# Moving when ScalarE's Silus run in a fused attention and feed-forward kernel, fixing ScalarE's order, and moving the state's decay to VectorE

## The chip, the cores and the metric

The kernel runs on one NeuronCore of one Trainium2 chip. The metric is the device time of one execution in microseconds (us), and I quote medians over several executions. Every execution that is compared here was in the fast state (no profile or time of a slower state came up).

The profile lists the work by engine. Four matter here, with their busy time before the change: TensorE for matrix products ("PE", 615.1 us, its weight loads listed apart as "PEld", 495.8 us), VectorE ("DVE", 498.4 us), ScalarE ("ACT", 286.6 us) and GpSimd ("POOL", 29.9 us). The trace shows for each its own sequence of instructions, and its waits for the others: ScalarE's Silus, for one, waited 30.9 us for sums of VectorE (L731).

## The reference

```python
def _attn_ref(q, k, v, f_logit):                     # batch 4, 8 heads, 768 steps, 48 per head
    f = 1.0 / (1.0 + np.exp(-f_logit))
    state = np.zeros((B, H, D, D), dtype=np.float32)
    for t in range(S):
        state = f[:, :, t, :, None] * state + np.einsum('bhd,bhe->bhde', k[:, :, t], v[:, :, t])
        y[:, :, t] = np.einsum('bhd,bhde->bhe', q[:, :, t], state)

def _moe_ref(x, w_gate, w_val, w_out):               # 3072 tokens, 384 -> 1536 -> 384
    g = x @ w_gate
    silu = g * (1.0 / (1.0 + np.exp(-g)))
    return silu * (x @ w_val) @ w_out
```

The attention's output, as 3072 rows of 384, is the x of the feed-forward block. All is float32.

## The kernel before

The sequence of 768 is cut into six chunks of 128 steps. The feed-forward part of chunk 0 multiplies plainly. Chunks 1 to 5 use two fast schemes that trade products for sums: a *triple* forms six gate/value blocks with fifteen products (four triples a chunk), and the output is formed with seven products. While the feed-forward part of chunk c runs, the attention of chunk c+1 (four batches) is worked off beside it; chunk 5 has none beside it.

Three places matter. The first is the attention step with the decay of the state and the Sigmoid of the gates:

```python
        if c >= SQUARES:
            nc.scalar.activation(squares("f"), squares("f"), AF.Sigmoid)                      # L510
        ...
        nc.vector.tensor_tensor_scan(tail[:, 0:n][:, ::-1], gate[:, 0:n][:, ::-1], ...)       # L519
        ...
            nc.gpsimd.tensor_tensor(decayed[:, :, 0:D], states[b], whole.broadcast_to(...), ALU.mult)   # L544
```

`decayed` is read by TensorE, and `whole`, the decay's factor, is a slice of the tile that the next scan writes; so that scan (L519) has to wait until the decay has read it (8 such waits in the trace, 5.0 us in all, the longest 0.69).

The second is the triple. `product(r)` makes two matmul calls, which the trace shows as four matmuls, into one of the PSUM banks A, B, o, c; bank B has one buffer and A has two, so a later product has to wait until ScalarE has copied the bank out (the trace has 8 such waits for B's copies into `aside`, 8.5 us in all, and 20 for A's, 6.5 us). `finish` applies Silu on ScalarE and then the product with the value half on VectorE:

```python
    def chained(made, f):
        n = len(traced)
        f()
        mine = [ins for ins in traced[n:] if ins.engine == mybir.EngineType.PE]
        keep_order(made[-1:] + mine)
        made.extend(mine)
    ...
        def triple(j):
            made, p, got = [], {}, {}
            ...
            def copy(name, tag, **kw):
                t = comb.tile([128, 2, TH], FP32, tag=tag, name=tag, **kw)
                nc.scalar.copy(t, p[name])
                return t

            def aside(name):
                return copy(name, "aside", bufs=3)

            def finish(i, n, src):
                dst = out_part(i, n, j)
                nc.scalar.activation(dst, src[:, 0, :], AF.Silu)
                nc.vector.tensor_tensor(dst, dst, src[:, 1, :], ALU.mult)

            def some(n, m):
                for r in range(n, m):
                    product(r)
                    if r == 0:
                        got[11] = copy("A", "c11", bufs=2)
                    # ... r = 1 to 4 cut: copies and sums
                    elif r == 5:
                        minus(got[12], p["o"], got[12])
                        finish(0, 1, got[12])
                    elif r == 6:
                        minus(got[22], got[22], aside("A"))
                        finish(1, 1, got[22])
                    # ... r = 7 to 11 cut
                    elif r == 12:
                        minus(got[31], got[31], aside("A"))
                        finish(2, 0, got[31])
                    elif r == 13:
                        plus(got[11], got[11], aside("B"))
                        finish(0, 0, got[11])
                    else:
                        finish(1, 0, p["A"])

            return [lambda n=n: chained(made, lambda: some(n, n + 5)) for n in (0, 5, 10)]
```

The third thing is that a scheduler of the compiler orders each engine's instructions before the run, from its own model of times. `keep_order` forbids it to reorder the instructions of the list; before the change that holds TensorE's products within a triple, and nothing on ScalarE.

Of the kernel before, what the change touches and what calls it, by code (L numbers as in the profile page):

```python
# [12 lines left out]
AF = mybir.ActivationFunctionType  # L13
ALU = mybir.AluOpType
# [275 lines left out]
def short_path(ctx, tc, ident, least, judge, q, k, v, f_logit, moe_w_gate, moe_w_val, moe_w_out, out):  # L290
# [9 lines left out]
    nc = tc.nc  # L300
    B, H, S, D = q.shape
    C = 128
    NCH = S // C
    HP = H // 2
# [57 lines left out]
    def pairs(t, off=0):  # L362
        return t[:, off:off + HP * N1].rearrange("p (a t) -> p a t", t=N1)
# [7 lines left out]
    states = [const.tile([128, HP, D], FP32, tag=f"state{b}", name=f"state{b}") for b in range(B)]  # L371

    decayed = const.tile([128, HP, W], FP32, tag="decayed", name="decayed")
# [114 lines left out]
    def rows_of(par):  # L488
        return slice(W * par, W * par + D)
# [6 lines left out]
    def attention(u):  # L496
        b, c = units[u]
# [4 lines left out]
        def transposed(name, src):  # L502
            p = bank(name)
            for a in range(HP):
                nc.tensor.transpose(p[:, a * C:(a + 1) * C],
                                    src[:, 2 * a:2 * a + 2, :].rearrange("t r d -> t (r d)"), ident)
            return p.rearrange("p (a t) -> p a t", t=C)
# [4 lines left out]
        else:  # L512
            p = transposed("fTp", fr)
# [4 lines left out]
        n = HP * N1  # L518
        nc.vector.tensor_tensor_scan(tail[:, 0:n][:, ::-1], gate[:, 0:n][:, ::-1], ones[:, ::-1], 1.0,  # L519
                                     op0=ALU.mult, op1=ALU.add)  # L520
        whole = pairs(tail)[:, :, 1:2]
# [19 lines left out]
        if c:  # L541
            if c < SQUARES:
                load_after(u)
            nc.gpsimd.tensor_tensor(decayed[:, :, 0:D], states[b], whole.broadcast_to((128, HP, D)), ALU.mult)  # L544
        yield

        A = att.tile([128, 2, HP, C], FP32, tag="A", name="A")
# [1 line left out]
        for a in range(HP):  # L549
            for par in range(2):  # L550
                r = rows_of(par)
# [4 lines left out]
        if c < NCH - 1:  # L556
            p = bank("kt")
# [8 lines left out]
        if c:  # L566
# [8 lines left out]
            for a in range(HP):  # L575
                for par in range(2):
                    r = rows_of(par)
# [9 lines left out]
            for h in range(H):  # L587
                a, par = h // 2, h % 2
                f = h * D
                while f < (h + 1) * D:  # L590
                    n = min((h + 1) * D, (f // 128 + 1) * 128) - f
                    r = W * (a % 2) + f - h * D
# [10 lines left out]
        if c < NCH - 1:  # L603
            p = bank("dS")
# [11 lines left out]
        if not c:  # L616
            p = bank("xTp")
# [5 lines left out]
    def load_after(u):  # L623

        w = u + (1 if units[u][1] >= SQUARES else 2)
        if w < len(units) and (units[w][1] >= SQUARES) == (w == u + 1):
            load(w)
# [8 lines left out]
    traced = nc.cur_bb.bb.instructions  # L636
# [9 lines left out]
    def keep_order(mine):  # L646
        for a, b in zip(mine, mine[1:]):
            tc.add_manual_dep(b, a.name, mybir.DependencyInfo(mybir.DependencyClass.NoSync,
                                                              mybir.DependencyReason.DATA), reason="order")
# [123 lines left out]
    def chained(made, f):  # L773

        n = len(traced)
        f()
        mine = [ins for ins in traced[n:] if ins.engine == mybir.EngineType.PE]
        keep_order(made[-1:] + mine)
        made.extend(mine)


    PRODUCTS = [("A", "a11", "t14"), ("B", "a23", "t8"), ("o", "a21", "b22"),
# [4 lines left out]

    def mlp_fifteen(c):
        h = {}
        b11, b12, b21, b22, b31, b32 = (xT[c][:, k, n * TH:(n + 1) * TH] for k in range(KT) for n in range(2))  # L790
        tokens = dict(b11=b11, b21=b21, b22=b22, b32=b32, t3=b31, t10=b12)

        def token_sums():
            x = comb.tile([128, 9, TH], FP32, tag="xs", name="xs")
            for n, nm in enumerate(("t14", "t15", "t8", "t9", "t2", "t1", "t4", "t11", "t5")):
                tokens[nm] = x[:, n, :]
            t = tokens
            minus(t["t14"], b21, b31)
            minus_both(t["t15"], b31, b32)
            plus(t["t8"], b21, t["t15"])  # L800
            plus(t["t9"], b12, b22)
            minus_both(t["t2"], t["t9"], t["t14"])
            plus(t["t1"], b12, b32)
            minus(t["t5"], b32, b11)
            plus(t["t4"], b11, t["t9"])
            minus_both(t["t11"], t["t4"], b21)
            plus(b12, b11, b12)
            plus(b31, b11, b31)

        w, e = weight_parts()  # L810
        weights_of = {f"a{i + 1}{k + 1}": t for (i, k), t in w.items()}
        weights_of.update({f"e{n}": t for n, t in enumerate(e)})

        def out_part(i, n, j):
            f = i * NJ + j
            if f % NP not in h:
                h[f % NP] = hidden_tile()
            return h[f % NP][:, 2 * (f // NP) + n, :]

        def triple(j):  # L820
            cols = slice(j * 128, (j + 1) * 128)
            made, p, got = [], {}, {}

            def both(name):
                return {"A": banks_a, "B": banks_b, "o": banks_o, "c": banks_o}[name].tile(
                    [128, 512], FP32, tag=name if name in "AB" else "o", name=name).rearrange("p (n t) -> p n t", n=2)

            def product(r):
                name, a, b = PRODUCTS[r]
                fresh = name == "o" or name not in p  # L830
                if fresh:
                    p[name] = both(name)
                for n in range(2):
                    nc.tensor.matmul(p[name][:, n, :], lhsT=weights_of[a][:, n, cols], rhs=tokens[b],  # L834
                                     start=fresh and n == 0, stop=True, skip_group_check=True)
# [8 lines that stand above are left out]

            def finish(i, n, src):

                dst = out_part(i, n, j)
                nc.scalar.activation(dst, src[:, 0, :], AF.Silu)  # L848
                nc.vector.tensor_tensor(dst, dst, src[:, 1, :], ALU.mult)  # L849

            def some(n, m):
                for r in range(n, m):
# [3 lines that stand above are left out]
                    elif r == 1:  # L856
                        got[22] = copy("B", "c22")
                    elif r == 2:
                        minus(got[22], p["o"], got[22])
                    elif r == 3:  # L860
                        got[12] = copy("A", "c12")
                    elif r == 4:
                        plus(got[12], got[12], aside("B"))
                    elif r == 5:
                        minus(got[12], p["o"], got[12])
                        finish(0, 1, got[12])
                    elif r == 6:
                        minus(got[22], got[22], aside("A"))
                        finish(1, 1, got[22])
                    elif r == 7:  # L870
                        got[32] = copy("B", "c32")
                    elif r == 8:
                        got[31] = copy("c", "c31")
                    elif r == 9:
                        plus(got[32], got[32], aside("A"))
                    elif r == 10:
                        minus(got[31], got[31], aside("B"))
                    elif r == 11:
                        minus(got[32], got[32], p["c"])
                        finish(2, 1, got[32])  # L880
# [5 lines that stand above are left out]
                        finish(0, 0, got[11])  # L886
                    else:
                        finish(1, 0, p["A"])

            return [lambda n=n: chained(made, lambda: some(n, n + 5)) for n in (0, 5, 10)]  # L890

        hidden_sums, last = down_seven(c, h)
        order = list(range(0, NJ, 2)) + list(range(1, NJ, 2))
        pieces = [token_sums] + [f for j in order for f in triple(j)]
        half = 1 + 3 * (NJ // 2)
        ready = [sorted({(i * NJ + j) % NP for i in range(KT) for j in range(n, NJ, 2)}) for n in range(2)]
        pieces.insert(half, lambda: [hidden_sums(n) for n in ready[0]])
        pieces.append(lambda: [hidden_sums(n) for n in ready[1]])
        return pieces, last

    def down_seven(c, h):
# [163 lines left out]
    for c in range(NCH):  # L1065
        if c == 0:
# [5 lines left out]
            pieces = hidden + weave(last, weight_sums(0))  # L1072
        else:
            hidden, last = mlp_fifteen(c)
            if c == 1:
                half = len(hidden) // 2
                hidden = hidden[:1] + weave(hidden[1:half], weight_sums(1)) + hidden[half:]
                hidden.append(lambda: behind(down_weight_sums))
            pieces = hidden + last
# [86 lines left out]
```

## Time and profile before

| | before |
|---|---|
| time, median | 644.23 us (643.03 to 645.19, 4 runs) |
| span of the profiled execution | 641.5 us |
| chunk 1 (fifteen-product part, seven-product part) | 105.9 (71.9, 34.0) us |
| chunk 2 | 102.6 (69.8, 32.9) us |
| chunk 3 | 102.2 (68.5, 33.7) us |
| chunk 4 | 96.3 (64.3, 32.0) us |
| chunk 5 | 80.1 (52.1, 28.0) us |

The lengths of the chunks are read between fixed landmarks of the trace: a chunk starts at the last output matmul of the chunk before it, and its two parts are divided at the first matmul of the seven-product scheme. This gives the same cut in every kernel, so the parts can be compared from run to run.

The table of busy time in stretches, for the fifteen-product parts of chunks 1 to 4 before the change (columns: stretch, length, then busy us of PE, PEld, DVE, ACT and POOL with counts, granted clock, DMA share, GB/s):

```profile
148.90:220.80 71.90, 66.85 (x447) 54.74 (x445) 70.80 (x127) 46.85 (x87) 1.86 (x3) 1.00 0.34 88
254.80:324.60 69.80, 66.09 (x444) 54.03 (x442) 55.51 (x100) 45.03 (x84) 1.34 (x2) 1.00 0.27 69
357.40:425.90 68.50, 65.43 (x443) 53.68 (x441) 55.26 (x99) 39.58 (x79) 1.03 (x2) 1.00 0.23 59
459.60:523.90 64.30, 62.11 (x383) 50.89 (x381) 53.07 (x99) 35.51 (x74) 1.82 (x3) 1.00 0.18 46
```

Take length minus PE for chunks 2 to 4: 3.71 + 3.07 + 2.19 = 8.97 us in which TensorE has nothing in it. In chunk 1 it is 5.05 us, and there VectorE is busy 70.80 of 71.90.

The group of the Silus, from the groups by line on ScalarE (after the last bar: idle time of ScalarE just before them, and for what):

```profile
L848 ACT ACTIVATE h<-c 128x256 f32<-128x256 f32 x100 | 40.4, 416 | 34.8 <-DVE c L731 30.9 <-DVE c L728 2.7
```

ScalarE stands 34.8 us in front of Silus whose input VectorE hasn't finished. A copy behind such a Silu stands as well: the one at 305.81 us starts after a Silu that has stood 3.57 us, though the matmuls of its product ended at 302.10.

### The profile page before, as it was taken

What the parts mean: (1) busy time and instruction counts of PE and PEld (TensorE: products, weight loads), DVE (VectorE), ACT (ScalarE), POOL (GpSimd) and SP (SyncE); (2) the same over time, 40 slices, a digit from 0 to 9 for tenths busy, and PEclk for the clock granted to TensorE, in tenths of its full rate; (3) what the DMA queues carried; (4) which work ended last, traced back from release to release, by engine and by line L of the source; (5) the groups of instructions that cost most, each with busy time, mean ns of one, the idle gap of its engine ahead of it and who ended that gap; (6) DMA issues with size and microseconds to landing.
All of it is one profiled execution on the core that took longest, in us unless ns stands there. A gap on an engine that the chain in (4) does not pass through costs nothing.

```text
span 641.5 us, 10613 instructions
## 1 busy us (share of the span) xinstructions
PE 615.1 (96%) x3894; PEld 495.8 (77%) x3894; DVE 498.4 (78%) x921; ACT 286.6 (45%) x526; POOL 29.9 (5%) x42
## 2 busy tenths in 40 slices
PE   7999999999998999999899999899999999999996
PEld 4954545667777799887689887689887789988896
DVE  6888879959999997679897589897679893467741
ACT  1474646205666511874640465461165540165600
POOL 1000000000000050000020000020000000000000
PEclk8999999999999999999999999999999999999999
DMA  9997475006133414113332313223402300100001
GB/s 176 216 221 239 118 188 172 14 17 190 30 83 92 98 44 113 43 40 80 79 79 71 99 29 84 62 67 87 120 26 50 75 9 7 62 1 1 0 1 54
DMA packets 98396, 51.90 MB, mean 81 GB/s; under 512 B 56864, under 2 KB 92192, under 8 KB 98336
## 3 DMA queue, kind: packets, MB, share of 16 engines
q1 hardware_dynamic: 95024, 46.63, 30.9%
q10 hardware_dynamic: 3312, 4.52, 2.0%
q8 instruction: 32, 0.52, 0.4%
q14 instruction: 28, 0.23, 0.1%
HBM read 42.47 MB, written 4.72 MB: 74 GB/s over the span
## 4 chain that ended last, share of the span: by engine, by line
PE 60%; DVE 19%; SPq 7%; DMA 5%; ACT 3%; issue 3%; POOL 0%; DVEq 0%; ACTq 0%; POOLq 0%
PE o L923 13%; PE A L834 9%; PE B L834 8%; SPq L593 5%; PE gate L666 5%; PE val L666 5%; PE sc L552 3%; PE o L834 3%; PE o L690 3%; DVE c L731 3%; PE c L834 2%; PE o L977 2%; PE y L582 2%; DMA ksquares<-in_k_dram 2%; DVE tails L519 1%
## 5 line engine op out<-in xcount | busy, mean ns | idle before, releaser
L834 PE MATMUL A<-xs,w_both 128*128 128x256 f32 x240 | 63.1, 383 | 3.6 <-ACT c L839 2.4
L923 PE MATMUL o<-w_out,h 128*128 128x192 f32 x360 | 62.6, 330 | 0.9 <-DVE w_out L731 0.4
L728 DVE TENSOR_TENSOR c<-c,aside 128x512 f32<-128x512 f32 x60 | 41.9, 698 | 26.8 <-ACT aside L839 26.7
L923 PEld LDWEIGHTS o<-w_out,h 128*128 128x128 f32 x360 | 58.1, 190 | 2.8 <-DVE w_out L731 0.6
L848 ACT ACTIVATE h<-c 128x256 f32<-128x256 f32 x100 | 40.4, 416 | 34.8 <-DVE c L731 30.9
L839 ACT COPY c<-A 128x512 f32<-128x512 f32 x40 | 23.3, 584 | 69.3 <-DMA out_dram<-ob 25.9
L839 ACT COPY aside<-A 128x512 f32<-128x512 f32 x60 | 35.2, 586 | 42.3 <-PE A L834 42.3
L834 PEld LDWEIGHTS A<-xs,w_both 128*128 128x128 f32 x240 | 44.2, 190 | 11.6 <-ACT c L839 4.1
L544 POOL TENSOR_TENSOR decayed<-state,tails 128x192 f32<-128x192 f32 x20 | 27.0, 1351 | 480.4 <-DVE state L610 331.7
L834 PE MATMUL B<-xs,w_both 128*128 128x256 f32 x160 | 42.6, 388 | 6.2 <-ACT aside L839 5.7
L731 DVE TENSOR_TENSOR c<-c,aside 128x512 f32<-128x512 f32 x60 | 41.7, 696 | 5.8 <-ACT aside L839 5.6
L849 DVE TENSOR_TENSOR h<-h,c 128x256 f32<-128x256 f32 x100 | 40.8, 421 | 5.9 <-ACT h L848 5.7
L834 PE MATMUL B<-xT,extra 128*128 128x256 f32 x160 | 41.3, 380 | 0.2 <-ACT aside L839 0.2
L834 PE MATMUL c<-xT,w_both 128*128 128x256 f32 x160 | 41.1, 379 | 0.0
L834 PE MATMUL A<-xs,extra 128*128 128x256 f32 x160 | 41.1, 379 | 0.0
L923 PE MATMUL o<-ws,h 128*128 128x192 f32 x240 | 40.9, 326 | 0.0
L839 ACT COPY aside<-B 128x512 f32<-128x512 f32 x60 | 35.0, 583 | 13.1 <-PE B L834 13.1
L923 PEld LDWEIGHTS o<-ws,h 128*128 128x128 f32 x240 | 39.1, 190 | 0.1
L834 PEld LDWEIGHTS B<-xs,w_both 128*128 128x128 f32 x160 | 29.0, 190 | 12.4 <-ACT aside L839 7.5
L519 DVE TENSOR_TENSOR_SCAN tails<-gates,ones 128x516 f32<-128x516 f32 x24 | 29.3, 1222 | 9.2 <-POOL decayed L544 5.0
L731 DVE TENSOR_TENSOR c<-o,c 128x512 f32<-128x512 f32 x40 | 27.8, 696 | 10.6 <-PE o L834 8.8
L552 PEld LDWEIGHTS sc<-qT,kT 48*128 48x128 f32 x384 | 25.0, 187 | 14.0 <-issue 10.0
(132 smaller groups left out, 1196.4 us busy)
## 6 DMA issues: line engine op xcount, KB each, us to landing
fsquares<-in_f_logit_dram SPq DMA_DIRECT2D x64, 96.0 KB, 2.4
ksquares<-in_k_dram SPq DMA_DIRECT2D x64, 96.0 KB, 2.4
qsquares<-in_q_dram SPq DMA_DIRECT2D x64, 96.0 KB, 2.4
v<-in_v_dram SPq DMA_DIRECT2D x24, 192.0 KB, 3.6
w<-in_moe_w_gate_dram SPq DMA_DIRECT2D x6, 768.0 KB, 4.6
w<-in_moe_w_val_dram SPq DMA_DIRECT2D x6, 768.0 KB, 5.4
w<-in_moe_w_out_dram SPq DMA_DIRECT2D x6, 768.0 KB, 5.4
out_dram<-ob ACTq DMA_DIRECT2D x23, 192.0 KB, 2.6
```

Of the source, the lines that this page charges most:

```text
L519: nc.vector.tensor_tensor_scan(tail[:, 0:n][:, ::-1], gate[:, 0:n][:, ::-1], ones[:, ::-1], 1.0, op0=ALU.mult, op1=ALU.add)
L544: nc.gpsimd.tensor_tensor(decayed[:, :, 0:D], states[b], whole.broadcast_to((128, HP, D)), ALU.mult)
L552: nc.tensor.matmul(sc[par][:, a * C:(a + 1) * C], lhsT=kT[r, a, :], rhs=qT[r, a, :], start=True, stop=True)
L593: nc.sync.dma_start(out=xT[c][f % 128:f % 128 + n, f // 128, b * C:(b + 1) * C], in_=yT[r:r + n, par, a // 2 * C:(a // 2 + 1) * C])
L666: nc.tensor.matmul(p, lhsT=w[:, i, j * 128:(j + 1) * 128], rhs=xT[c][:, i, :], start=(i == 0), stop=(i == KT - 1))
L728: nc.vector.tensor_tensor(dst, a, b, ALU.add)
L731: nc.vector.tensor_tensor(dst, a, b, ALU.subtract)
L834: nc.tensor.matmul(p[name][:, n, :], lhsT=weights_of[a][:, n, cols], rhs=tokens[b], start=fresh and n == 0, stop=True, skip_group_check=True)
L839: nc.scalar.copy(t, p[name])
L848: nc.scalar.activation(dst, src[:, 0, :], AF.Silu)
L849: nc.vector.tensor_tensor(dst, dst, src[:, 1, :], ALU.mult)
L923: nc.tensor.matmul(p[:, n, :], lhsT=lhsTs[j][:, n * C:(n + 1) * C], rhs=rhs[:, j, :], start=first and j == 0 and n == 0, stop=j == NP - 1, ...
```

## The change

The intent is that ScalarE never meets a Silu whose input isn't ready. `finish` now only notes the Silu and its product in a list; one of them is taken from the list after a copy, some products later, at fixed places (`r in (3, 5, 6, 7, 9, 10)`), if need be in the next triple. ScalarE's instructions of the triples are kept in the order in which they are written, so that the scheduler can't put the Silus ahead again, and the chain of order runs over the whole chunk. The decay (L544) goes from GpSimd to VectorE.

```diff
-            nc.gpsimd.tensor_tensor(decayed[:, :, 0:D], states[b], whole.broadcast_to((128, HP, D)), ALU.mult)
+            nc.vector.tensor_tensor(decayed[:, :, 0:D], states[b], whole.broadcast_to((128, HP, D)), ALU.mult)
@@ chained
-        mine = [ins for ins in traced[n:] if ins.engine == mybir.EngineType.PE]
-        keep_order(made[-1:] + mine)
-        made.extend(mine)
+        for engine in (mybir.EngineType.PE, mybir.EngineType.Activation):
+            mine = [ins for ins in traced[n:] if ins.engine == engine]
+            keep_order(made.get(engine, []) + mine)
+            made[engine] = mine[-1:] or made.get(engine, [])
@@ mlp_fifteen
+        made, late = {}, []
@@ triple
-            made, p, got = [], {}, {}
+            p, got = {}, {}
@@ finish
-                dst = out_part(i, n, j)
-                nc.scalar.activation(dst, src[:, 0, :], AF.Silu)
-                nc.vector.tensor_tensor(dst, dst, src[:, 1, :], ALU.mult)
+                def f():
+                    dst = out_part(i, n, j)
+                    nc.scalar.activation(dst, src[:, 0, :], AF.Silu)
+                    nc.vector.tensor_tensor(dst, dst, src[:, 1, :], ALU.mult)
+                late.append(f)
@@ some: finish(0, 1, ...) and finish(1, 1, ...) move from r == 5 and r == 6 to r == 8
+                    if r in (3, 5, 6, 7, 9, 10) and late:
+                        late.pop(0)()
@@ end of mlp_fifteen
+        def finish_late():
+            while late:
+                late.pop(0)()
-        pieces.insert(half, lambda: [hidden_sums(n) for n in ready[0]])
-        pieces.append(lambda: [hidden_sums(n) for n in ready[1]])
+        pieces.insert(half + 2, lambda: [hidden_sums(n) for n in ready[0]])
+        pieces.append(lambda: (chained(made, finish_late), [hidden_sums(n) for n in ready[1]]))
```

More of the change, by code (lines that the diff above doesn't have):

```diff
@@ L865, in some @@
                         minus(got[12], p["o"], got[12])
-                        finish(0, 1, got[12])
                     elif r == 6:
                         minus(got[22], got[22], aside("A"))
-                        finish(1, 1, got[22])
                     elif r == 7:
@@ L873, in some @@
                         got[31] = copy("c", "c31")
+                        finish(0, 1, got[12])
+                        finish(1, 1, got[22])
                     elif r == 9:
```

## The prediction

> **What bounds the kernel now.** I read the page first, then the table by stage, the waits of the weight load, and the timeline around the longest of those waits. On the page TensorE is busy 96% of the span and VectorE 78%:
>
> ```profile
> PE 615.1 (96%) x3894; PEld 495.8 (77%) x3894; DVE 498.4 (78%) x921; ACT 286.6 (45%) x526; POOL 29.9 (5%) x42
> ```
>
> The kernel does six chunks of tokens. The first multiplies plainly; the five others use a scheme of fifteen products per triple, four triples a chunk, then a scheme of seven products for the output. Chunks 1 to 4 also carry the attention of the next chunk; chunk 5 carries none. The table of busy time in stretches, one per chunk from 140 us on (columns: length, then busy us of PE, PEld, DVE, ACT, POOL, then clock, DMA share, GB/s), shows what each is bound by:
>
> ```profile
> 140.00:256.00 116.00, 109.96 (x719) 92.12 (x718) 108.34 (x202) 54.80 (x101) 11.10 (x5) 1.00 0.35 90
> 256.00:358.00 102.00, 98.12 (x679) 84.55 (x678) 81.36 (x155) 51.12 (x95) 5.70 (x4) 1.00 0.29 75
> 358.00:459.50 101.50, 97.65 (x678) 84.28 (x677) 81.25 (x154) 45.79 (x90) 5.38 (x4) 1.00 0.28 70
> 459.50:556.20 96.70, 94.28 (x604) 81.23 (x603) 68.73 (x136) 37.72 (x79) 1.84 (x3) 1.00 0.15 41
> 556.20:608.20 52.00, 52.00 (x240) 44.90 (x239) 34.60 (x67) 32.61 (x66) 0.00 (x0) 1.00 0.02 5
> ```
>
> The last row is the clean case: 60 products in 52.0 us, 0.87 us each, TensorE never idle. Chunks 2 to 4 are TensorE's as well, with a few us lost. In chunk 1 VectorE is busy 108.3 of 116 us, because it also forms sums of weights: there VectorE is nearly the bound. So the change can win only what TensorE loses to waits. Those are best read at the weight load, which sits ahead of each matmul:
>
> ```profile
> PEld B L834 <- ACT aside L839: 8.5, 8, 2.9
> PEld A L834 <- ACT aside L839: 6.5, 20, 0.9
> PEld A L834 <- ACT c L839: 4.1, 5, 1.2
> PEld o L977 <- DVE ob L728: 3.8, 5, 1.2
> PEld sc L552 <- DVE qT L540: 2.7, 2, 2.4
> PEld B L834 <- ACT c L839: 0.9, 1, 0.9
> ```
>
> (us in all, times, longest.) Nearly all are products (L834) that wait for ScalarE to copy their bank out (L839). ScalarE is busy 45%, so it isn't short of time; it is held. The timeline at the longest wait shows by what (start, duration, instruction; in brackets the idle time before it and its releaser):
>
> ```profile
> 302.27 0.51 POOL L544 TENSOR_TENSOR decayed<-state,tails 128x192 f32<-128x192 f32 x1 [18.38 <-DVE state L610]
> ...
> 302.82 1.23 DVE L519 TENSOR_TENSOR_SCAN tails<-gates,ones 128x516 f32<-128x516 f32 x1 [0.69 <-POOL decayed L544]
> ...
> 304.17 0.68 DVE L731 TENSOR_TENSOR c<-c,aside 128x512 f32<-128x512 f32 x1
> 304.77 0.68 DVE L731 TENSOR_TENSOR c<-c,c 128x512 f32<-128x512 f32 x1
> ...
> 305.48 0.42 ACT L848 ACTIVATE h<-c 128x256 f32<-128x256 f32 x1 [3.57 <-DVE c L731]
> ...
> 305.81 0.57 ACT L839 COPY aside<-B 128x512 f32<-128x512 f32 x1
> ...
> 306.42 0.73 PEld L834 LDWEIGHTS B<-xs,w_both 128*128 128x128 f32 x4 [2.87 <-ACT aside L839]
> ```
>
> VectorE waits 0.69 us for GpSimd's decay, then runs a 1.23 us scan. Only then does it update c, for which the Silu at the head of ScalarE's sequence has stood 3.57 us. The copy behind that Silu needs none of this: its product was done. TensorE waits 2.87 us for the copy.
>
> [...] the same decay takes 512 ns at the least and 8732 ns at the most, the long one beside a full VectorE. [...] the nearest row in the trace, the state's sum L610, takes 349. [...]
>
> **The change part by part.** I also compared the order of instructions of both kernels on each engine.
>
> Decay. Twenty instructions leave GpSimd; VectorE gets 20 x 0.35 = 7.0 us. In return VectorE loses its waits for the decay: "tails <- decayed" is 5.0 us in the waits (8 times, up to 0.69). Net +2 us on VectorE, four fifths of it in chunks where VectorE is busy 70 to 80%. It comes off the front of the stall above, 0.69 - 0.35 = 0.34 us. Worth near nothing alone.
>
> Silus later. Nothing is added or removed; 120 Silus (0.42 us) and 120 products on VectorE (0.42 us) move. By the new order the copies of the thirteenth and fourteenth products no longer stand behind a Silu, and the Silus of the last four results stand in the next triple, one behind each copy, their inputs long ready. So the stalls in which a Silu held a copy go. I add those with such a Silu in front, in the weight load's idle time: chunk 2 has 2.9 + 0.9, chunk 3 has 2.0 + 0.9 + 0.9, chunk 4 has 1.8 + 1.2: 10.6 us. I count three quarters, 8.0 us, since VectorE's backlog stays and may hold another copy.
>
> What stays of the rest of the ACT waits (8.5 + 6.5 + 4.1 + 0.9 = 20.0). The 20 waits of the fifteenth product for the copy of the thirteenth, 4.8 us (group A<-xT,w_both, 0.24 each), are in the algorithm: both use one bank and only one product lies between. Chunk 5 shows them too. The waits of about 1 us at 319 and 421 us follow a Sigmoid with its table load (1.28 + 0.63 us) ahead of a copy; the Sigmoid is not moved by the change's rule, so they stay, some 2 us. In chunk 1 there are 2.9 us of such waits and 2.7 for qT, but VectorE there has only 116 - 108.3 = 7.7 us free; I count 1.0 us.
>
> What it costs. The new program has two more table loads in this path (30 against 28), as a Silu now can stand between two Sigmoids: 2 x 1.28 us of ScalarE, of which I put half on the path, 1.3. Also, at each chunk's end four Silus come after the last copy: 4 x 0.42 = 1.7 us on ScalarE, then the VectorE products. The output's first products take 12 x 0.34 = 4.1 us and need the third of these only at the fourth pair (2.1 us in), so they just about hide; 0.1 us a chunk, 0.5.
>
> Sum: 8.0 + 1.0 + 0.3 - 1.3 - 0.5 = 7.5 us gained. 645.0 - 7.5 gives 637.5; I say **637.5 us**, 1.2% faster.
>
> **The rivals.**
> 1. A new wait takes the old one's place. c22, c31 and c32 have one buffer each. The old reader is now a late product on VectorE, so the copy into c31 waits for a product issued only three products earlier, 3 x 0.87 = 2.6 us, while VectorE's backlog was seen at over 3 us. Then ScalarE stands at that copy instead of at a Silu, and TensorE behind it. For it: the new order has such waits ("c31 copy waits for h"). Against it: the Silus' inputs are ready early, so most slack is kept. It would give back 3 to 6 us: 641 to 644.
> 2. The Sigmoids become the hold. With the sequence fixed, attention's copies and Sigmoids fall where they fall; in the new order one stands between the copies of the thirteenth and fourteenth products of a triple and one ahead of the next triple's first copy. Each costs up to 1 us, at most 12 of them: 640 to 645. The trace shows three such today.
> 3. VectorE becomes the bound in chunk 1, by 4 x 0.35 more decay and late products: that chunk stays at 116 or gains 2 us more waits. Time 639 to 641.
> 4. All waits but the structural ones go, and chunk 1 shortens too, by 5 us: 645 - 10.6 - 2 - 5 = 627. Only then is it over 2% (below 632.1). I think TensorE's own floor speaks against it: chunks 2 to 4 lose 102.0 - 98.1 + 101.5 - 97.7 + 96.7 - 94.3 = 10.1 us of idle matmul time in all, some for other reasons.
>
> **Range and chances.** Low end 631: all 10.6 us and 3 in chunk 1. High end 644: rival 1 or 2 in full. Faster by over 2% needs 12.9 us of the some 15 that are not structural: 0.13. Slower by over 2% needs 658, thirteen us of new stalls: 0.03. Within 2%: 0.84.
>
> **What would show it.** Right: "B <- aside" falls from 8.5 to under 3 us, and "A <- c" from 4.1 to under 2; no Silu with over 2 us of idle time before it in chunks 2 to 4; the fifteen-product part of chunks 2 and 3 each shorter by some 3 us; chunk 5 unchanged at 52 us for its products; the decay on VectorE near 350 ns, GpSimd empty. Wrong by rival 1: ScalarE copies of c31, c32 or c22 idle "<- DVE h". By rival 2: waits of 1 us right behind Sigmoids. By rival 3: chunk 1 no shorter, VectorE over 109 us busy in it. The prediction would fail most if chunk 1, where the order changes most and I count least, moves by over 4 us either way.

## The result, and the profile after

| | before | after |
|---|---|---|
| time, median | 644.23 us | 633.95 us (632.15 to 634.8, 4 runs) |
| ratio of fast runs | 1 | 0.9838 (95% interval 0.9808 to 0.9867) |
| span of the profiled execution | 641.5 us | 632.1 us |
| chunk 1 (fifteen, seven) | 105.9 (71.9, 34.0) | 108.4 (73.9, 34.5) |
| chunk 2 | 102.6 (69.8, 32.9) | 98.0 (65.1, 32.9) |
| chunk 3 | 102.2 (68.5, 33.7) | 97.5 (65.0, 32.5) |
| chunk 4 | 96.3 (64.3, 32.0) | 93.7 (61.9, 31.8) |
| chunk 5 | 80.1 (52.1, 28.0) | 80.2 (52.1, 28.1) |

A ratio here is the mean time of one kernel's fast runs over the mean of the other's in the same rounds; it is therefore not quite the ratio of the medians. The changed kernel is 1.6% faster, which at a threshold of 2% counts as the same. The gain lies in chunks 2 to 4: 4.6 + 4.7 + 2.6 = 11.9 us. Chunk 1 became 2.5 us longer, chunk 5 didn't move.

The busy line of the page, after:

```profile
PE 616.3 (98%) x3894; PEld 499.3 (79%) x3894; DVE 500.1 (79%) x941; ACT 288.1 (46%) x528; POOL 2.9 (0%) x22
```

GpSimd is empty (29.9 us before); its twenty instructions are now among VectorE's 941 (921 before). TensorE's share rises because the span shrinks.

The same four stretches as before, after the change:

```profile
149.00:222.90 73.90, 69.66 (x447) 56.51 (x445) 71.22 (x132) 47.49 (x87) 0.00 (x0) 0.98 0.32 85
...
257.40:322.50 65.10, 64.97 (x443) 54.06 (x442) 54.75 (x101) 42.87 (x83) 0.00 (x0) 1.00 0.29 75
...
355.40:420.40 65.00, 64.86 (x443) 54.33 (x441) 53.68 (x97) 39.83 (x79) 0.00 (x0) 1.00 0.24 62
...
452.80:514.70 61.90, 61.90 (x383) 51.33 (x381) 52.67 (x99) 38.54 (x76) 0.00 (x0) 1.00 0.21 56
```

In chunks 2 to 4 length minus PE is now 0.13 + 0.14 + 0.00: of 8.97 us of empty TensorE 0.27 is left. The parts became shorter by 10.6 us, more than those 8.7. The rest is in the PE column itself, which falls from 193.63 to 191.73. A reason is visible in the stall that the prediction shows: the weight load stood 2.87 us, but the matmul record after it counts only 2.46 as idle (it also lasts 1.13 us instead of 1.03 for the same four matmuls). So the busy time of PE hides 0.41 us of this stall; the weight load's wait, or the length of the stretch, shows it whole.

The weight load's waits after, for the same groups (us in all, times, longest):

```profile
PEld A L836 <- ACT aside L841: 3.9, 14, 0.4
PEld B L836 <- ACT aside L841: 2.6, 7, 0.7
PEld o L988 <- DVE ob L728: 2.1, 4, 0.7
...
PEld A L836 <- ACT c L841: 0.2, 1, 0.2
```

The waits for ScalarE's copies were 8.5, 6.5, 4.1 and 0.9 us, 20.0 together; they are 3.9, 2.6 and 0.2, 6.7 together. The longest was 2.9 us and is 0.7.

The Silus' group after, from the groups by line:

```profile
L852 ACT ACTIVATE h<-c 128x256 f32<-128x256 f32 x100 | 41.7, 419 | 2.1 <-DVE c L728 1.5 <-DVE c L731 0.4
```

Their idle time went from 34.8 to 2.1 us with the busy time unchanged. How that comes about is best seen where the two kernels do the same work: the end of the triple that holds the 2.87 us stall of before. The timeline there, after:

```profile
303.40 0.36 DVE L544 TENSOR_TENSOR decayed<-state,tails 128x192 f32<-128x192 f32 x1
...
303.79 1.23 DVE L519 TENSOR_TENSOR_SCAN tails<-gates,ones 128x516 f32<-128x516 f32 x1
...
304.86 0.59 ACT L841 COPY aside<-B 128x512 f32<-128x512 f32 x1 [0.43 <-PE B L836]
...
305.25 0.68 DVE L731 TENSOR_TENSOR c<-c,c 128x512 f32<-128x512 f32 x1
305.85 0.69 DVE L731 TENSOR_TENSOR c<-c,aside 128x512 f32<-128x512 f32 x1
306.18 0.84 PEld L836 LDWEIGHTS B<-xs,w_both 128*128 128x128 f32 x4
```

The scan still takes 1.23 us, and VectorE still updates c only at 305.25 and 305.85. But the copy at 304.86 no longer stands behind a Silu that needs them; ScalarE even waits 0.43 us for the product. The weight load of the next triple's second product, at 306.18, follows with no idle time. VectorE's lateness is still there, and nothing that TensorE needs stands behind it any more.

The decay, from the view of its tile, before and after (minimum, median and maximum in ns; first and last start):

```profile
L544 POOL TENSOR_TENSOR decayed<-state,tails x20: 512/518/8732, 42.9 to 523.1; 128x192 f32<-128x192 f32 x20
```

```profile
L544 DVE TENSOR_TENSOR decayed<-state,tails x20: 327/358/434, 51.0 to 517.6; 128x192 f32<-128x192 f32 x20
```

One thing in chunk 1 isn't the change. The table of stretches around 200 us, after:

```profile
199.00:200.00 1.00, 0.31 (x4) 0.32 (x6) 1.00 (x3) 0.00 (x0) 0.00 (x0) 1.00 0.76 201
...
202.00:203.00 1.00, 1.00 (x4) 0.75 (x3) 1.00 (x4) 0.48 (x1) 0.00 (x0) 0.50 0.34 69
```

TensorE's weight load had waited 2.18 us for qT up to 199.7; from 200.9 to 204.3, for 3.41 us, the granted clock is half (0.50). Half of 3.41 us, an estimated 1.7 us, is lost by that. The profile of before had a wait of 2.38 us at the same place and no such stretch. A second profile of the changed kernel (e10 below) has no such stretch either: there the fifteen-product part of chunk 1 is 1.5 us shorter (72.4 against 73.9), but the seven-product part is 0.8 longer (35.3 against 34.5), so of the 2.5 us by which chunk 1 is longer here only 0.7 are gone. The half-clock stretch is in some profiles and not in others (more on it at the end).

### The profile page after: what moved, and what is told of

It reads as the page before. It is cut to its first block, busy times and chain, and to the rows that moved or that the text cites. A ratio compares the mean times of both kernels' runs of the same rounds, so it can differ in the third digit from the quotient of the medians.

```text
span 632.1 us, 10566 instructions
## 1 busy us (share of the span) xinstructions
PE 616.3 (98%) x3894; PEld 499.3 (79%) x3894; DVE 500.1 (79%) x941; ACT 288.1 (46%) x528; POOL 2.9 (0%) x22
## 4 chain that ended last, share of the span: by engine, by line
PE 81%; DVE 8%; SPq 3%; DMA 3%; ACT 2%; issue 2%; DVEq 0%; ACTq 0%
PE o L934 17%; PE A L836 13%; PE B L836 11%; PE gate L666 5%; PE val L666 5%; PE c L836 4%; PE o L836 4%; PE sc L552 4%; PE o L988 3%; PE o L690 3%; PE y L582 3%; SPq L593 3%; PE y L578 2%; PE kt L559 1%; DVE c L731 1%
## 5 line engine op out<-in xcount | busy, mean ns | idle before, releaser
L836 PEld LDWEIGHTS A<-xs,w_both 128*128 128x128 f32 x240 | 45.5, 192 | 6.8 <-ACT aside L841 0.4
L853 DVE TENSOR_TENSOR h<-h,c 128x256 f32<-128x256 f32 x100 | 42.1, 432 | 8.2 <-ACT h L852 8.2
L852 ACT ACTIVATE h<-c 128x256 f32<-128x256 f32 x100 | 41.7, 419 | 2.1 <-DVE c L728 1.5
L841 ACT COPY aside<-B 128x512 f32<-128x512 f32 x60 | 35.0, 584 | 10.7 <-PE B L836 10.5
L554 DVE TENSOR_TENSOR A<-sc,causal 128x512 f32<-128x512 f32 x48 | 31.1, 686 | 5.9 <-PE sc L552 5.9
L836 PEld LDWEIGHTS B<-xT,extra 128*128 128x128 f32 x160 | 29.9, 190 | 6.2 <-ACT aside L841 2.1
L586 ACT COPY yT<-y 128x256 f32<-128x256 f32 x40 | 14.4, 372 | 43.7 <-PE y L582 36.7
```

Of the source, the lines that this page charges most:

```text
L554: nc.vector.tensor_tensor(A[:, par], sc[par].rearrange("p (a t) -> p a t", t=C), causal.unsqueeze(1).broadcast_to((128, HP, C)), ALU.mult)
L836: nc.tensor.matmul(p[name][:, n, :], lhsT=weights_of[a][:, n, cols], rhs=tokens[b], start=fresh and n == 0, stop=True, skip_group_check=True)
```

## The experiments

The theory after the first look: the gain needs the late Silus *and* the fixed sequence together, and the decay gives little. The rivals: one of the two alone does it; the decay does much of it; chunk 1 hides a loss that can be undone. All runs below are of five rounds, in three groups of four; the kernel before had medians of 645.49, 645.23 and 645.28 us in them. All outputs were correct.

| run | median us (range) | ratio to before (95%) |
|---|---|---|
| e1_decay_only | 642.51 (641.48 to 643.15) | 0.9952 (0.9932 to 0.9971) |
| e2_late_gpsimd | 636.97 (635.90 to 637.61) | 0.9870 (0.9849 to 0.9891) |
| e3_hold_only | 657.10 (655.91 to 659.18) | 1.0176 (1.0153 to 1.0199) |
| e4_late_free | 641.83 (640.43 to 642.18) | 0.9938 (0.9919 to 0.9958) |
| e5_chunk1_old | 634.48 (633.95 to 635.37) | 0.9832 (0.9810 to 0.9854) |
| e6_no_sigmoid | 1744.09 (1742.39 to 1747.60) | 2.7042 (2.6987 to 2.7098) |
| e7_sums_gpsimd | 635.52 (635.09 to 636.23) | 0.9855 (0.9833 to 0.9877) |
| e8_bunched | 635.24 (633.82 to 635.95) | 0.9848 (0.9827 to 0.9870) |
| e10_after_again | 634.18 (632.50 to 635.77) | 0.9835 (0.9821 to 0.9849) |
| e9_tanh | 630.34 (628.92 to 631.33) | 0.9766 (0.9751 to 0.9780) |
| e11_own_whole | 638.32 (636.13 to 639.87) | 0.9893 (0.9875 to 0.9911) |
| e12_chain_only | 642.21 (641.63 to 642.90) | 0.9949 (0.9935 to 0.9963) |

### The decay alone: e1_decay_only

The kernel before, with one line changed.

```diff
-            nc.gpsimd.tensor_tensor(decayed[:, :, 0:D], states[b], ...
+            nc.vector.tensor_tensor(decayed[:, :, 0:D], states[b], ...
```

> The kernel before with one change: the decay on VectorE. Theory (the late Silus are the gain): 643 to 645 us, within 1.5 us of the kernel before; the 5.0 us of 'tails <- decayed' go, but the Silus still hold copies and 'B <- aside' stays at 7 us or more. Rival [...]: 638 to 641.

Twenty small instructions moved give 0.48%, 3.0 us (between 1.9 and 4.4), ten times what the prediction put down. The stalls of the Silus are still there:

```profile
L848 ACT ACTIVATE h<-c 128x256 f32<-128x256 f32 x100 | 40.3, 416 | 33.7 <-DVE c L731 31.2 <-DVE c L728 1.5
```

33.7 us against 34.8, so the decay doesn't act through them. The weight load's wait "B <- aside" went from 8.5 to 7.2.

### All but the decay: e2_late_gpsimd

The changed kernel with the decay back on GpSimd.

```diff
-            nc.vector.tensor_tensor(decayed[:, :, 0:D], states[b], ...
+            nc.gpsimd.tensor_tensor(decayed[:, :, 0:D], states[b], ...
```

> The changed kernel with the decay back on GpSimd. Theory: 633 to 636 us, within 1.5 us of the changed kernel, with all of the gain in chunks 2 to 4. Rival (the decay matters): 638 or more, scans of VectorE waiting for the decay again.

0.9870 is 8.4 us of gain without the decay. The two parts add up roughly: 8.4 + 3.0 = 11.4 us, against the 10.4 to 10.7 of the whole change (ratios 0.9838 and 0.9835). By chunks, this profile is shorter than before by 3.2, 3.2 and 2.9 us in chunks 2 to 4, 9.3 us, and longer by 1.9 in chunk 1, here without a half-clock stretch there. What the decay on GpSimd costs now shows elsewhere, in the weight load's waits of this run:

```profile
PEld o L988 <- DVE ob L728: 5.4, 5, 1.7
```

This is 2.1 us after the change. It's the seven-product part: its last products wait for a bank that VectorE reads out, and VectorE is later there. The seven-product parts of chunks 1 to 4 take 134.2 us here and 131.7 after (132.4 in e10, the changed kernel's second profile, where the waits for `ob` are 2.8 us).

### The fixed sequence alone: e3_hold_only

The changed kernel with each Silu at once in place of being noted, and ScalarE held to that order (two of the six stand at r == 8, as in the changed text, in place of 5 and 6).

```diff
-                late.append(f)
+                f()
@@
-        pieces.insert(half + 2, lambda: [hidden_sums(n) for n in ready[0]])
+        pieces.insert(half, lambda: [hidden_sums(n) for n in ready[0]])
```

> The changed kernel with every Silu and product at once where it stood before, but TensorE and ScalarE held to that sequence. Theory (lateness is what frees the copies): the Silus stand in front of the copies again, so at least as slow as the kernel before, 644 to 652 us, with Silus idle for VectorE's c by 25 us or more. Rival (the fixed sequence is the gain, because the scheduler had put copies badly): 634 to 638.

This is the strongest result of the study: 1.8% slower than before, and 2.2% (14 us) slower than e1, from which it differs in the hold, the longer chain and the place of those two Silus. The groups by line, and the timeline at one of the stalls:

```profile
L852 ACT ACTIVATE h<-c 128x256 f32<-128x256 f32 x100 | 39.9, 415 | 72.0 <-DVE c L731 55.5 <-DVE c L728 16.4
```

```profile
311.34 0.42 ACT L852 ACTIVATE h<-c 128x256 f32<-128x256 f32 x1 [3.92 <-DVE c L731]
...
311.66 0.57 ACT L841 COPY aside<-A 128x512 f32<-128x512 f32 x1
...
312.28 0.73 PEld L836 LDWEIGHTS A<-xT,w_both 128*128 128x128 f32 x4 [2.51 <-ACT aside L841]
```

ScalarE's wait before Silus doubles to 72.0 us. At 311.34 the Silu has stood 3.92 us for VectorE, the copy behind it follows at 311.66, and TensorE gets its bank 2.51 us late. It's the stall of before, more often: held to the written order, ScalarE meets more Silus whose input isn't ready than in the order that the scheduler had chosen freely.

### The late Silus alone: e4_late_free

The changed kernel without the hold on ScalarE.

```diff
-        for engine in (mybir.EngineType.PE, mybir.EngineType.Activation):
+        for engine in (mybir.EngineType.PE,):
```

> The changed kernel with late Silus, but only TensorE held to the sequence; ScalarE is left to the scheduler. Theory: the lateness does most of it, 634 to 639 us. Rival (without the hold the scheduler moves Silus ahead of copies again): 641 to 645, Silus idle for VectorE's c by 20 us or more.

0.9938, and the decay alone was 0.9952: lateness in the program's text by itself gives 0.9 us, within the intervals of both. Its Silus' group:

```profile
L852 ACT ACTIVATE h<-c 128x256 f32<-128x256 f32 x100 | 41.1, 418 | 24.0 <-DVE c L731 21.7 <-DVE c L728 1.3
```

24.0 of 34.8 us are still there. Writing an instruction later doesn't place it later: in this trace Silus whose input isn't ready (up to 2.8 us of wait) stand ahead of copies again, presumably because the scheduler's model takes the input to be ready; the model itself isn't seen here. So neither part works alone; the hold is what keeps the late places late.

### The longer chain of order: e12_chain_only

The change also makes the chain of TensorE's order run over the whole chunk instead of one triple. This is e1 with that alone.

```diff
     def mlp_fifteen(c):
         h = {}
+        made = []
@@
-            made, p, got = [], {}, {}
+            p, got = {}, {}
```

> As e1 (the kernel before with the decay on VectorE), and TensorE's products chained through a whole chunk instead of a triple; Silus and ScalarE as before. Theory (the longer chain is neutral): within 1 us of e1's ratio of 0.9952. If it is slower by 2 us or more, then e4's late Silus alone were worth that much more than their ratio of 0.9938 says, and e3's loss is partly the chain's.

0.9949 against 0.9952: the chain is neutral, and the difference between e3 and e1 belongs to ScalarE's hold with the two moved Silus, which no run takes apart. The later place of the sums of h (`half + 2`) wasn't run alone either.

### Where the late Silus stand: e8_bunched

All noted Silus at two places instead of one at each of six.

```diff
-                    if r in (3, 5, 6, 7, 9, 10) and late:
-                        late.pop(0)()
+                    if r in (3, 9):
+                        while late:
+                            late.pop(0)()
```

> The changed kernel with the late Silus in bunches (four after the fourth product, two after the tenth) instead of one per copy. Theory (a Silu whose input is ready costs only its own 0.42 us, and a bunch of four is 1.7 us against some 0.85 us of slack of a bank): each triple loses up to 0.6 us at the eighth product, 3 to 12 us in all, 637 to 645. Rival (lateness alone matters, spacing does not): 633 to 635.

0.9848 against 0.9835, intervals overlapping, and chunks 2 to 4 within 0.5 us of the changed kernel. ScalarE's idle time before these Silus is 5.6 us instead of 2.1 and costs nothing that the time shows. That there is one Silu per copy isn't what matters; that their inputs are long ready is.

### The changed kernel again: e10_after_again

> The changed kernel itself once more, so that the next three are compared with it on the same chip: 633 to 636 us, ratio to the kernel before 0.982 to 0.986 under any theory. A ratio of 0.988 or more would say that the 2 to 3 us put down to single parts are within what the chip's runs scatter.

0.9835, as the first measurement. In its profile there is no half-clock stretch in the middle of the run; chunk 1 is 107.7 us there and the span 630.8 us, against 108.4 and 632.1. So 1.8 us of chunk 1's lengthening over before stay when the clock is whole.

### Chunk 1 in the old manner: e5_chunk1_old

Chunk 1 gets immediate Silus, free ScalarE, a chain per triple and its sums at the old place; chunks 2 to 5 stay as changed (core of the edit).

```diff
+        whole, late, held = {}, [], c > 1
+        engines = (mybir.EngineType.PE, mybir.EngineType.Activation)[:1 + held]
...
-                late.append(f)
+                late.append(f) if held else f()
...
-        pieces.insert(half + 2, lambda: [hidden_sums(n) for n in ready[0]])
+        pieces.insert(half + 2 * held, lambda: [hidden_sums(n) for n in ready[0]])
```

> The changed kernel with chunk 1 alone in the old manner (Silus at once, ScalarE free, sums of h where they were), chunks 2 to 5 as changed. Chunk 1 was 2.5 us longer in the changed kernel (105.9 to 108.4). Theory A (late products in the chunk that VectorE bounds cost it): chunk 1 back to 106 us, whole time 631 to 632.5. Theory B (it is the decay on VectorE and a stretch of half clock after a 2.2 us wait, both of which stay): chunk 1 stays at 107 to 108, whole time 633 to 635.

0.9832 against 0.9835: undoing the change in chunk 1 gains nothing. Its profile has chunk 1 at 107.3 us, with a half-clock stretch at 202.6 us, and chunk 2 at 99.2, 1.2 us longer than in the changed kernel. What chunk 1 may lose is given back in chunk 2; the time doesn't separate them.

### Taking load off VectorE in chunk 1: e7_sums_gpsimd

Nine of the sixteen sums of weights that fall in chunk 1 go from VectorE to GpSimd.

```diff
+    def plus_aside(dst, a, b):
+        nc.gpsimd.tensor_tensor(dst, a, b, ALU.add)
+    def minus_aside(dst, a, b):
+        nc.gpsimd.tensor_tensor(dst, a, b, ALU.subtract)
@@
-        return [lambda f=f, d=d, x=x, y=y: f(d, x, y) for f, d, x, y in (
+        on_gpsimd = {plus: plus_aside, minus: minus_aside}
+        return [lambda f=on_gpsimd[f] if odd and i > 6 else f, d=d, x=x, y=y: f(d, x, y) for i, (f, d, x, y) in enumerate((
```

> The changed kernel with nine of the sixteen sums of weights in chunk 1 on GpSimd, which is idle there. VectorE loses 9 x 0.69 = 6.2 us of work in the first half of chunk 1. Theory (VectorE bounds chunk 1): chunk 1 shorter by 3 to 5 us, 629 to 631 us. Rival [...]: the sums come late, TensorE waits for them at half of the chunk, 640 or more.

Both expectations missed. The sums weren't late on GpSimd (1.3 to 2.2 us each, all done by 182.7 us), and chunk 1 wasn't shorter either: 109.8 us, with a longest wait of the scores for qT of 3.8 us, and a half-clock stretch from 182.3 us right behind it. The time is 0.9855, not told apart from the changed kernel's. The timeline shows why:

```profile
177.87 1.44 POOL L734 TENSOR_TENSOR w_both<-w_both 128x512 f32<-128x512 f32 x1
178.11 1.75 DVE L728 TENSOR_TENSOR c<-c,aside 128x512 f32<-128x512 f32 x1
...
180.04 1.48 DVE L540 TENSOR_TENSOR qT<-qT,head 128x512 f32<-128x512 f32 x1
...
181.58 1.15 PEld L552 LDWEIGHTS sc<-qT,kT 48*128 48x128 f32 x16 [3.84 <-DVE qT L540]
```

Both VectorE instructions take 0.69 us in the median elsewhere in this trace. Seven VectorE instructions beside the sums on GpSimd are over 0.1 us longer than their kind's median, 6.2 us in all, which is as much as the nine sums had cost VectorE; its busy time even rose, from 500.1 to 501.8 us, with nine instructions fewer. So this run didn't relieve VectorE: that VectorE bounds chunk 1 is neither shown nor excluded by it, and I have no experiment that shortened chunk 1. What bounds it stays open.

### Sigmoids without a table: e6_no_sigmoid, a failed experiment

To price the table loads I replaced the Sigmoid in the later chunks by a copy with a scale, wrong on purpose.

```diff
-            nc.scalar.activation(squares("f"), squares("f"), AF.Sigmoid)
+            nc.scalar.activation(squares("f"), squares("f"), AF.Copy, scale=0.45)
```

> The changed kernel with a scaled copy in place of the 16 Sigmoids of the later chunks, wrong on purpose: no table is loaded for them, and ScalarE is freed of some 20 loads of 1.28 us and is never held by one. Theory (with Silus out of the way little of TensorE's time waits for ScalarE): 1 to 2.5 us faster than the changed kernel, 'B <- aside' from 2.6 to under 1. Rival 2 (Sigmoids and their loads are now the hold): 5 us or more faster.

It took 1744 us, for a reason that I hadn't thought of. Some gates became negative, so the smallest product of gates fell below the limit that this kernel itself checks, and its flag sent the data through the general path afterwards as well. (That also made the output correct, as the general path computed all again.) The time says nothing. In the trace's first part, chunk 5 ended at 621.4 us instead of 626.7, a hint of 5.3 us; the next run does it properly.

### A Sigmoid that needs no table of its own: e9_tanh

sigmoid(x) = 0.5 tanh(x/2) + 0.5. In this run's trace neither the Tanh nor the scaled copy has a load of its own (none of the path's 8 is at their lines), so two passes (0.63 us each in the mean) stand in the place of a pass and its table loads (1.28 us each).

```diff
-            nc.scalar.activation(squares("f"), squares("f"), AF.Sigmoid)
+            nc.scalar.activation(squares("f"), squares("f"), AF.Tanh, scale=0.5)
+            nc.scalar.activation(squares("f"), squares("f"), AF.Copy, scale=0.5, bias=0.5)
```

> The changed kernel with the later chunks' Sigmoid computed as half of a tanh plus a half (a Tanh and a scaled copy, both in the table that Silu uses), a correct result: 8 table loads in place of 30 in this path, one more pass of 0.63 us a unit. The attempt with no Sigmoid ended its chunks 5.3 us earlier in the trace. Theory: the loads hold copies, so 3 to 5 us faster than the changed kernel, 629 to 631 us. Rival: the second pass takes back what the loads cost, under 1 us.

It's correct, 0.9766 against 0.9835 on the same chip: 4.4 us faster than the changed kernel, and 2.3% faster than before. It beats both kernels. ScalarE's timeline from 160 us on, first of the changed kernel, then of this one:

```profile
161.67 0.42 ACT L852 ACTIVATE h<-c 128x256 f32<-128x256 f32 x1
162.10 1.28 ACT L510 ACT_TABLE_LOAD   x1
163.40 0.63 ACT L510 ACTIVATE fsquares<-fsquares 128x512 f32<-128x512 f32 x1
...
165.00 1.28 ACT L852 ACT_TABLE_LOAD   x1
```

```profile
161.65 0.42 ACT L853 ACTIVATE h<-c 128x256 f32<-128x256 f32 x1
161.97 0.61 ACT L510 ACTIVATE fsquares<-fsquares 128x512 f32<-128x512 f32 x1
...
164.51 0.42 ACT L853 ACTIVATE h<-c 128x256 f32<-128x256 f32 x1
164.82 0.62 ACT L511 ACTIVATE fsquares<-fsquares 128x512 f32<-128x512 f32 x1
```

The Sigmoid here cost a load on the way in and one on the way back, 1.28 us each; there were 30 loads in all in this path, and now there are 8. ScalarE was far from full (46% busy after the change), so why is it worth 4.4 us? The weight load's waits for ScalarE's copies hardly differ between the two (6.7 and 6.0 us). The gain lies in chunks 2 to 4, which take 96.0, 96.0 and 92.6 us, 4.6 less together than after the change. I counted in both traces how TensorE changes there between the feed-forward products and the attention's small matmuls. It changes over and back 36 times after the change and 28 times here. The time from the last product's start to the first small matmul's start sums to 10.5 and 8.0 us, that from the last small matmul's start to the next product's start to 6.4 and 4.6 us: 4.3 us less at these changes, of the 4.6. (Steps between products became 0.8 us more in all, those between small matmuls 1.0 less.) So with the table loads attention's blocks were cut up more often, and the time at the cuts is of the size of the gain, although the table of stretches showed TensorE empty for only 0.27 us there. In chunk 1 the ways back fall from 15 to 9 and from 4.6 to 1.3 us, but the chunk is hardly shorter (107.9 against 108.4 us, and 107.7 in e10). This is read from the traces; no run varied the number of changes by itself, so that the cuts are the cause is argued and not shown.

### What about the decay costs so much: e11_own_whole

If the decay costs through the scan that must wait for it, then a copy of its factor of its own frees the scan, and GpSimd can keep the work. This is e2 with that.

```diff
+            own = att.tile([128, HP, 1], FP32, tag="own", name="own", bufs=2)
+            nc.vector.tensor_copy(own, whole)
+            nc.gpsimd.tensor_tensor(decayed[:, :, 0:D], states[b], own.broadcast_to((128, HP, D)), ALU.mult)
```

> Late Silus with the decay on GpSimd, as e2, but GpSimd reads a small copy of its factor (128x4, 0.17 us on VectorE), so that the next scan need not wait for the decay. Theory (the decay cost its 2 to 3 us through that wait): 634 to 635 us, as the changed kernel. Rival [...]: 636 to 638, as e2.

The scan's waits for the decay (5.0 us before, 3.6 in e2) are gone from the trace, and the time is 0.9893, no better than e2 and by the ratios 3.7 us behind the changed kernel on the same chip. The rival holds: it isn't the scan's wait. (The twenty copies add a little work to VectorE, which e1's form doesn't.) What the decay does to VectorE's instructions beside it stays a candidate. The mean of the sums c<-c,aside doesn't show it (698 ns with an empty GpSimd, 696 in e2), but single instructions of VectorE beside a decay are lengthened, as here in e2, where the same product takes 0.42 us in the median:

```profile
478.72 1.01 POOL L544 TENSOR_TENSOR decayed<-state,tails 128x192 f32<-128x192 f32 x1 [35.92 <-PE y L578]
...
479.28 0.73 DVE L853 TENSOR_TENSOR h<-h,c 128x256 f32<-128x256 f32 x1
```

Those that are over 0.1 us longer than their kind's median sum to 1.6 us before the change, 2.0 in e2 and 3.2 in e11. Besides, the decay itself comes late, 822 ns in the median and up to 3133 here, 588 and up to 1911 in e2, 358 and at most 434 on VectorE, and the waits for `ob` in the seven-product part go with it (5.0 here, 5.4 in e2, 2.1 and 2.8 in the two profiles of the changed kernel). By which chain the one leads to the other, and how much falls to each, I haven't shown.

## Why the prediction was right or wrong

The time was predicted as 637.5 us and measured as 633.95, inside the range and in the class that had most of the chance. The mechanism was the right one; several terms of the sum were mis-sized, and their errors partly cancelled, so that part of the number's nearness is luck.

- **The stalls with a Silu in front go: right, under-sized.** The prediction counted 8.0 us, because VectorE's backlog stays. The backlog stays, as the timeline shows, but nothing of TensorE's stands behind it. Without the decay (e2) chunks 2 to 4 gained 9.3 us in the profiles. Both halves of the change are needed for it (e3 and e4), which the prediction didn't take apart.
- **The signs it named came.** "B <- aside" fell to 2.6 us (under 3 was said), "A <- c" to 0.2 (under 2), no Silu of chunks 2 to 4 has over 2 us in front of it (2.1 us for all 100), the fifteen-product parts of chunks 2 and 3 lost 4.7 and 3.5 us (some 3 was said), chunk 5's products took 52.1 us as before, the decay 358 ns (near 350), GpSimd is empty.
- **The decay "worth near nothing alone", 0.3 us: wrong.** It's worth 3.0 us alone (e1) and some 2.3 us on top of the rest (e2, 0.9870, against e10, 0.9835; from two groups of runs, so only to within some 2 us). The term was taken from one stall, 0.69 - 0.35 us, and the way by which it acts isn't that stall (e11). The prediction had the tell-tale number in hand, durations from 512 to 8732 ns for the same instruction, and didn't price it. Its 7.0 us of new work on VectorE came (20 of 358 ns), but VectorE's busy time rose by only 3.8 us in e1 (498.4 to 502.2), in part because its own instructions became shorter: the two groups of sums c<-c,aside went from 698 and 696 ns in the mean to 690 and 688. Before the change all of those that were over 0.1 us longer than their kind's median (1.6 us in all) ran beside an instruction of GpSimd; in the profile after it there are none.
- **Chunk 1 gains 1.0 us: wrong in sign.** It's 1.8 us longer with a whole clock (e10), 2.5 with the half-clock stretch. The prediction named chunk 1 as its weakest place and its rival 3 said 2 us more waits there. But VectorE is busy only 0.4 us more in that part, e5 didn't win the time back, and e7 didn't relieve VectorE, so rival 3 is neither shown nor excluded. Why chunk 1 lost stays open.
- **Two more table loads, 1.3 us, and "some 2 us" for the Sigmoids that stay:** the count of loads is right (30), the price of the Sigmoids is too low: doing without their loads wins 4.4 us in spite of 16 more passes of some 0.62 us (e9). Rival 2 looked for it as waits of 1 us behind Sigmoids. It doesn't appear as waits; the traces suggest attention blocks cut up.
- **Chunk ends, 0.5 us:** not seen; the seven-product parts of chunks 1 to 4 take 131.7 and 132.4 us in the two profiles after and 132.6 before. No run isolates it.
- **Rival 1, a new wait in place of the old:** it's there once, a copy into c31 that waits 1.8 us for h (in chunk 1), so rightly set aside. Double buffers for c22, c31 and c32 weren't tried.
- **Rival 4, all stalls go, 627 us:** half of it came. The empty TensorE time of chunks 2 to 4 did go almost whole (8.97 to 0.27 us), against the prediction's judgement that some of it had other reasons, and e9 then took 4.6 us more out of these chunks; the 5 us in chunk 1 didn't come.

With the sizes that were measured in the traces the sum would have been 9.3 (Silus, with the new loads in it) + 2.6 (decay, e2 to after in chunks 2 to 4) - 1.8 (chunk 1) = 10.1 us. The medians differ by 10.3. These terms come from the same traces, so this checks the bookkeeping and not the causes.

## What to carry to other kernels

If an engine with spare time holds up the bound engine, look at what stands in front of the instruction that is waited for: here ready copies stood behind Silus that waited for VectorE. Put instructions with late inputs behind those with early ones, and fix that order if a scheduler decides it, but never fix an order before it's a good one: the same hold gained some 6.5 us with late Silus (e4 to after) and cost 14 us without them (e1 to e3). Price a small instruction by its spread, not by its median, and look at single instructions rather than means before calling another engine free: nine sums on an idle GpSimd gave VectorE back nothing (e7, 500.1 us busy became 501.8). A table switch may cost more by what it does to its neighbours' order than by the waits that show: in e9 the time fell by 4.4 us and the waits for ScalarE's copies by only 0.7 (that the order is the cause was argued and not shown).

## What the traces show of the hardware

- In the first profile of the changed kernel a weight load's wait of 2.18 us (up to 199.7 us; the matmul column is idle for 1.78 of it) was followed by 3.41 us at half clock, from 200.9 us. The length of the wait alone doesn't decide it: the second profile of the same code (e10), with a wait of 2.2 us, hasn't the stretch, and the kernel before waited 2.38 us at that place without it.
- In e9 a Tanh follows a Silu without a load (161.65 and 161.97 us), while in the changed kernel the Sigmoid at the same place has one before it and the next Silu another, 1283 ns each (30 loads became 8, and 4.4 us). In ScalarE's timeline above the load starts 0.01 us after the Silu's end and the Sigmoid 0.02 us after the load's.
- The decay, one instruction of 192 elements in 128 partitions, took from 512 to 8732 ns on GpSimd (before) and 327 to 434 on VectorE (after). VectorE's instructions were lengthened beside GpSimd's, up to 1.75 us in place of 0.69 (e7).
- At the changes on TensorE between 128-row products and small attention matmuls, in chunks 1 to 4 after the change, it's 0.31 us in the median from a product's start to the first small matmul's, and 0.20 us from the last small matmul's start to the next product's, where products follow each other every 0.22 us.
